# PSUM banks for batch 0's attention: two groups of four by turns in place of one ring of seven

## The chip, the core and the metric

The kernel runs on one core of one Trainium2 chip. The metric is the device time of one execution in microseconds (us): the median of the runs. Lower is better. The engines are called as in the profile: PE (TensorE), DVE (VectorE), ACT (ScalarE), POOL (GpSimd), SP (SyncE, which issues the transfers). PSUM, the memory that PE writes its products to, is used as eight banks, k0 to k7.

## What is computed

Attention over 8 batches of 8 heads (576 positions, 64 wide), and a feed-forward layer on its result:

```python
q_d, k_d, v_d = (t.reshape(B, H, S // 4, 4, D).mean(axis=3) for t in (q, k, v))
out_up = np.repeat(sm_attn(q_d, k_d, v_d), 4, axis=2)     # softmax attention on means of 4 positions
scores = np.where(abs(i - j) < 4, q @ k.T / 8, -1e9)      # and attention on the 7 nearest positions
out_local = softmax(scores) @ v
x = (out_up + out_local) as 4608 rows of 512              # rows: batch by batch; columns: heads
h = x @ w_in                                              # 512 -> 2048
out = (s * np.maximum(h, 0) ** 2 + b) @ w_out             # 2048 -> 512
```

A row of x needs all heads of its batch, so the feed-forward layer can't start on a batch before all of its attention is done.

## The kernel before

**The feed-forward part** takes 18 tiles of 256 rows (t) and 8 slices of 256 hidden columns (p). `gemm1(t, p)` writes 24 products of x with a slice of w_in into one bank (ph, L556 to L558: both factors are split in a high and a low part, and three of the four products are taken); ACT and DVE then make the squared result in two parts (L566 to L569), and `gemm2(t, p)` adds 12 products with a slice of w_out (po, L601 to L603). The steps run in the order of a list: t = 0 and 1 by turns for p = 0 to 6, then t = 2 for p = 0 to 6, then p = 7 of the three, then t = 3 to 17. A gemm2 is written two steps behind its gemm1. Tile t = 2 holds the end of batch 0 and the start of batch 1, so its first gemm1 needs the whole attention of batch 1.

**The weights** are 64-bit numbers, which ACT and DVE turn into a high and a low part in `convert` (L226 to L234). Slices p = 0 to 6 have a staging buffer each in turn; slice 7 (`load_quarter`, L211) comes in eight quarters: load, L226 on ACT, L227 to L230 on DVE, L231 on ACT, L234 on DVE. A quarter's load reuses the buffer of the quarter ahead, so it can't start before that quarter's L230.

**Attention of batches 0 to 2** goes by pairs of heads, four a batch, each in `first_unit`. A pair takes eight PSUM tiles in this order: sa (products of the averaged q and k, L303), sl twice (the near scores, one head each, L383 and L388), tp and tr (transposes, L322 to L327), up (L337, L339), ol twice (L431). On the way the softmax of sa goes over DVE L304, ACT L305, L307, L311, DVE L312, ACT L314; that of sl over DVE L393, L394, ACT L397, DVE L398 to L401 (batch 0: L401 on POOL), DVE L411 and ACT L414 four times; L434 on DVE adds ol and up into x. `split_x` (L542 on ACT, L543 on DVE) makes x's high and low part, xh and xl, for gemm1. A bank is handed on when the reader of its tile is done.

**Banks.** Each pair draws its tiles from a ring, the next tile from the next bank. Batch 0 uses one ring of k0 to k3 and k5 to k7 for all four pairs. The rings of batch 1 (k5, k6) and 2 (k5) are small, since gemm1 and gemm2 hold the others: ph of t = 0 is in k4, that of t = 1 in k7 for p under 7, po of t = 0, 1, 2 in k0 and k1, k2 and k3, k6 and k7.

**The order of the instructions** isn't the order in which the functions are called. A scheduler builds each engine's queue from a model of the run: it takes what its model has ready, the attention of batches 0 to 2 ahead of the rest (`tc.high_priority`). Each engine then runs its own queue strictly in order, so an instruction that waits holds back all that stand behind it on that engine. One changed bank thus moves instructions on all engines.

Of the kernel before, what the change touches and what calls it, by code (L numbers as in the profile page):

```python
# [62 lines left out]
def attention_ffn_kernel(ctx, tc, qk, vw_in, vr_in, vdm, qkn, vn, w_in, w_out, s_in, b_in, out):  # L63
# [8 lines left out]
    def bank(i, shape, name):  # L72
        return ps.tile(shape, F32, tag=f"k{i}", name=name)
# [109 lines left out]
    def clear(i):  # L183
        da, vm = room[i]["dg"], room[i]["sc"][:, 1536:1792]
        n = 2 * NG * P
        for j in range(0, n + QV, 488):
            nc.gpsimd.memset(da[:, j : min(j + 488, n + QV)], 0.0)
        nc.gpsimd.memset(vm, 0.0)
        diag[i] = (take(da, 0, [P, 2 * NG, P]), *blocks(da, n, vm))
# [431 lines left out]
    def banks(*ids):  # L621
        ring = itertools.cycle(ids)
        return lambda shape, name: bank(next(ring), shape, name)

    def load_ahead(i):
        for j in range(i, min(i + 3, EU)):
            load_pair(*units[j])
# [7 lines left out]
    sb_b = cst.tile([P, 1], F32, name="sb_b")  # L635
    nc.sync.dma_start(sb_b, bass.AP(b_in.tensor, b_in.offset, [[0, P], [1, 1]]))
    clear(1)
    bk = banks(0, 1, 2, 3, 5, 6, 7)
    for hp in range(HP):
        load_ahead(hp)  # L640
        if hp > 1:
            clear(hp)
        with tc.high_priority(offset=400):
            for _ in first_unit(0, hp, bk):
                pass
    split_w(0)
    load_w(1)
# [122 lines left out]
```

## Time and profile before

| | |
| --- | --- |
| device time, median of 3 runs | 971.38 us (971.03 to 973.79) |
| the profiled execution | 972.49 us, its span 970.7 us |
| busy share of the span: PE, DVE, ACT, POOL | 97%, 66%, 49%, 43% |
| granted PE clock | 1.00 of full in the whole span |
| DVE busy from 30 to 69.2 us | 37.97 of 39.2 us |
| PE busy from 30 to 69.2 us | 27.95 of 39.2 us |
| PE busy from 69.2 to 160 us | 90.80 of 90.8 us |

The program has two stretches. Up to about 69 us all engines work on batch 0's attention, and on the first weights; PE waits for the others. After that PE runs the feed-forward part, with the attention of later batches strewn in, almost without a gap to the end. In the timeline rows the columns are start, duration, engine, line, operation, tiles (written <- read), and in brackets the idle time of the engine just ahead and what ended it. Durations of neighbours on one engine overlap by some hundredths to tenths of a microsecond, so what a row costs its queue is the distance to the next start. The profile counts an fp32 product of PE as two (12 rows of ol are x24).

### The profile page before, as it was taken

How to read it: one execution, taken by the hardware profiler on the slowest of the kernel's cores; microseconds unless marked ns; L12 is line 12 of the kernel's file. 1: busy time of each engine (PE TensorE's matmuls, PEld its weight loads, DVE VectorE, ACT ScalarE, POOL GpSimd, SP SyncE). 2: the span in 40 equal slices, each digit the busy share in tenths (PEclk: the TensorE clock that was granted, in tenths of full speed). 3: DMA queues.
4: the chain of work that ended last, by engine and by line, in shares of the span. 5: the costliest groups of instructions: out<-in, count | busy, mean ns of one | idle time of the engine just before them, and what ended most of it. 6: DMA issues, size and time to landing. Idle time of an engine off the chain costs nothing.

```text
span 970.7 us, 18541 instructions
## 1 busy us (share of the span) xinstructions
PE 938.7 (97%) x7316; PEld 843.4 (87%) x7316; DVE 637.7 (66%) x1175; ACT 475.0 (49%) x1141; POOL 418.0 (43%) x455
## 2 busy tenths in 40 slices
PE   5769999999999999999999999999999999999998
PEld 4559988888999999998888899989899999998987
DVE  5999996864567878787787878787878521211121
ACT  5878775553754453545363545453635433333231
POOL 9421011101066686776868786867676200000000
PEclk9999999999999999999999999999999999999999
DMA  9736512112243232323241424242412000000000
GB/s 316 261 121 210 172 60 78 49 42 73 101 134 113 77 110 72 102 70 133 67 136 66 135 68 131 72 134 69 136 55 76 1 22 1 23 1 22 1 23 22
DMA packets 32103, 86.26 MB, mean 89 GB/s; under 512 B 3344, under 2 KB 7952, under 8 KB 32016
## 3 DMA queue, kind: packets, MB, share of 16 engines
q1 hardware_dynamic: 32016, 85.08, 26.6%
q8 instruction: 57, 0.93, 0.4%
q14 instruction: 30, 0.25, 0.1%
HBM read 75.63 MB, written 9.44 MB: 88 GB/s over the span
## 4 chain that ended last, share of the span: by engine, by line
PE 74%; DVE 9%; DMA 8%; POOL 5%; ACT 2%; issue 2%; SPq 0%; DVEq 0%; ACTq 0%; POOLq 0%
PE ph L556 11%; PE ph L557 11%; PE ph L558 11%; PE po L603 11%; PE po L601 11%; PE po L602 11%; DMA tqk<-in_qk_dram 3%; POOL pr L466 3%; POOL acc L488 3%; DMA wst<-in_moe_w_out_dram 2%; PE sa L303 2%; DVE bias L579 1%; PE up L339 1%; PE ol L431 1%; DMA lqk<-in_qkn_dram 1%
## 5 line engine op out<-in xcount | busy, mean ns | idle before, releaser
L556 PE MATMUL ph<-xh,wi 128*128 128x256 f32 x1152 | 325.4, 283 | 3.7 <-ACT xh L542 2.5
L557 PE MATMUL ph<-xl,wi 128*128 128x256 f32 x1152 | 323.9, 281 | 0.0
L558 PE MATMUL ph<-xh,wi 128*128 128x256 f32 x1152 | 323.6, 281 | 0.0
L466 POOL TENSOR_TENSOR pr<-lqk 128x576 f32<-128x576 f32 x140 | 201.2, 1461 | 73.2 <-DMA lqk<-in_qkn_dram 29.2
L556 PEld LDWEIGHTS ph<-xh,wi 128*128 128x128 f32 x1152 | 217.5, 189 | 11.2 <-ACT xh L542 2.8
L557 PEld LDWEIGHTS ph<-xl,wi 128*128 128x128 f32 x1152 | 217.4, 189 | 5.4 <-issue 0.2
L558 PEld LDWEIGHTS ph<-xh,wi 128*128 128x128 f32 x1152 | 217.6, 189 | 0.3
L566 ACT ACTIVATE ph<-ph 128x512 f32<-128x512 f32 x144 | 83.8, 582 | 229.0 <-PE ph L558 223.2
L601 PE MATMUL po<-wo,gh 128*128 128x512 f32 x456 | 180.7, 396 | 0.0
L602 PE MATMUL po<-wo,gh 128*128 128x512 f32 x456 | 180.5, 396 | 0.0
L603 PE MATMUL po<-wo,gl 128*128 128x512 f32 x456 | 177.9, 397 | 0.0
L569 DVE TENSOR_TENSOR gl<-ph,gh 128x512 fp32r<-128x512 f32 x114 | 77.8, 683 | 115.8 <-ACT gh L568 115.5
L488 POOL TENSOR_TENSOR acc<-acc,pv 128x576 f32<-128x576 f32 x80 | 114.4, 1430 | 57.1 <-DVE acc L488 29.5
L468 DVE TENSOR_REDUCE st<-pr 128x9 f32<-128x576 f32 x140 | 105.9, 757 | 37.7 <-POOL pr L466 35.4
L292 POOL TENSOR_TENSOR dq<-vq 64x64 f32<-64x64 f32 x58 | 22.8, 393 | 197.4 <-PE up L337 195.3
L603 PEld LDWEIGHTS po<-wo,gl 128*128 128x128 f32 x456 | 85.7, 188 | 17.6 <-issue 0.2
L487 DVE TENSOR_TENSOR pv<-lv,st 128x576 f32<-128x576 f32 x120 | 87.5, 747 | 18.8 <-POOL acc L488 18.4
L601 PEld LDWEIGHTS po<-wo,gh 128*128 128x128 f32 x456 | 85.7, 188 | 15.9 <-ACT gh L568 0.6
L602 PEld LDWEIGHTS po<-wo,gh 128*128 128x128 f32 x456 | 85.7, 188 | 15.8
L568 ACT CAST gh<-ph 128x512 fp32r<-128x512 f32 x114 | 66.9, 587 | 64.3 <-PE po L602 62.4
L567 ACT ACTIVATE ph<-ph 128x512 f32<-128x512 f32 x144 | 83.7, 582 | 3.2
L602 PE MATMUL po<-wo,gb 128*128 128x512 f32 x120 | 47.1, 392 | 0.0
(149 smaller groups left out, 1239.3 us busy)
## 6 DMA issues: line engine op xcount, KB each, us to landing
tqk<-in_qk_dram SPq DMA_DIRECT2D x30, 584.0 KB, 4.1
lqk<-in_qkn_dram SPq DMA_DIRECT2D x20, 768.0 KB, 4.2
lv<-in_vn_dram SPq DMA_DIRECT2D x20, 480.0 KB, 3.4
out_dram<-os SPq DMA_DIRECT2D x17, 512.0 KB, 3.1
wst<-in_moe_w_in_dram SPq DMA_DIRECT2D x7, 1024.0 KB, 6.5
wst<-in_moe_w_out_dram SPq DMA_DIRECT2D x7, 1024.0 KB, 5.3
tvd<-in_vdm_dram SPq DMA_DIRECT2D x29, 160.0 KB, 2.9
tvr<-in_vr_dram SPq DMA_DIRECT2D x29, 128.0 KB, 3.1
```

The source lines that it names most:

```text
L466: nc.gpsimd.tensor_tensor(pr, lqk[:, 0:CH], lqk[:, CH + o : 2 * CH + o], ALU.mult)
L468: nc.vector.tensor_reduce(ls[:, :, o], pr, AX.X, ALU.add)
L487: nc.vector.tensor_tensor(pv, lv[:, o : o + CH], w, ALU.mult)
L488: (nc.vector if o % 3 == 1 else nc.gpsimd).tensor_tensor(acc[:, :, h], acc[:, :, h], pv, ALU.add)
L556: nc.tensor.matmul(ph[:, j], wi[p][:, 0, k, f], xh[:, k], start=(k == 0), stop=False)
L557: nc.tensor.matmul(ph[:, j], wi[p][:, 0, k, f], xl[:, k], start=False, stop=False)
L558: nc.tensor.matmul(ph[:, j], wi[p][:, 1, k, f], xh[:, k], start=False, stop=(k == NK - 1))
L566: nc.scalar.activation(ph, ph, AF.Relu)
L567: nc.scalar.activation(ph, ph, AF.Square)
L601: nc.tensor.matmul(po[m], gh[:, j, ms], wo[p][:, 0, j], start=first, stop=False)
L602: nc.tensor.matmul(po[m], gh[:, j, ms], wo[p][:, 1, j], start=False, stop=False)
L603: nc.tensor.matmul(po[m], gl[:, j, ms], wo[p][:, 0, j], start=False, stop=last)
```

## The change

Batch 0's pairs 0 and 2 draw their eight tiles from a ring of k0 to k3, pairs 1 and 3 from one of k4 to k7. A pair has four banks in place of seven, but shares them with one other pair only, and k4, unused by batch 0 before, is taken as well. No instruction is added or removed.

```diff
-    bk = banks(0, 1, 2, 3, 5, 6, 7)
+    bks = [banks(0, 1, 2, 3), banks(4, 5, 6, 7), banks(0, 1, 2, 3), banks(4, 5, 6, 7)]
     for hp in range(HP):
 ...
-            for _ in first_unit(0, hp, bk):
+            for _ in first_unit(0, hp, bks[hp]):
```

The queues change from their first few instructions to the last gemm1 of t = 2; behind that they are the same, instruction by instruction. Three places follow; numbers behind a name tell buffers apart, and x3 means three equal rows.

**PE, around the first gemm1.** `ph<-xh,wi` (L556) is its first product. In the rows before, tp, tr, up and ol with the names pd, ptr, dq, db are those of batch 1's first pair; ol<-flat is batch 0's last.

```order
L322 MATMUL tp<-ident,pd 80x96
L325 MATMUL tp<-ident,pd 80x96 x2
L327 MATMUL tr<-ident,pd 64x96 x3
L337 MATMUL up<-ptr,dq 128x144
L339 MATMUL up<-ptm,dq 128x144 x2
L431 MATMUL ol<-flat 64x96 x12
L556 MATMUL ph<-xh,wi 128x256
L431 MATMUL ol<-db,tvw 64x96 x12
L557 MATMUL ph<-xl,wi 128x256
```

The same place with the change:

```order
L431 MATMUL ol<-flat 64x96 x12
L383 LDWEIGHTS idb
L383 MATMUL sl<-maskb,idb 128x192
L388 MATMUL sl<-tqk 32x32 x24
L556 MATMUL ph<-xh,wi 128x256
L322 MATMUL tp<-ident,pd 80x96
L325 MATMUL tp<-ident,pd 80x96 x2
L556 MATMUL ph<-xh,wi 128x256
L557 MATMUL ph<-xl,wi 128x256
```

Batch 1's first pair has only sa and sl ahead of the first gemm1 now; its tr, up and ol stand further back among gemm1 and gemm2, and the pairs after it are all later too.

**PE, the end of batch 1's last pair** (up_1925, ol_1931 and ol_1951 are its tiles; ph_2127 is gemm1 of t = 1, p = 6). Before, it is strewn among the feed-forward products:

```order
L601 MATMUL po_1068<-wo_1581,gh_1919 128x512
L337 MATMUL up_1925<-ptr_1885,dq_139 128x144
L339 MATMUL up_1925<-ptm_1883,dq_139 128x144 x2
L602 MATMUL po_1068<-wo_1581,gh_1919 128x512
...
L556 MATMUL ph_2127<-xh_751,wi_1698 128x256
L431 MATMUL ol_1931<-db_146,tvw_1088 64x96 x6
L557 MATMUL ph_2127<-xl_752,wi_1698 128x256
L558 MATMUL ph_2127<-xh_751,wi_1698 128x256
L556 MATMUL ph_2127<-xh_751,wi_1698 128x256
L431 MATMUL ol_1951<-db_146,tvw_1088 64x96 x6
```

With the change (ph_2179 is the first gemm1 of t = 2, sa_2334 the first tile of batch 2; the rows ahead of these are the last gemm2 of p = 6 with sa_1755 and sl_1766 of the pair among them):

```order
L383 LDWEIGHTS idb_120
L383 MATMUL sl_1825<-maskb_122,idb_120 128x192
L388 MATMUL sl_1825<-tqk_1082 32x32 x24
L322 MATMUL tp_1875<-ident_75,pd_1753 80x96
L325 MATMUL tp_1875<-ident_75,pd_1753 80x96 x2
L327 MATMUL tr_1876<-ident_75,pd_1753 64x96 x3
L337 MATMUL up_1925<-ptr_1885,dq_139 128x144
L339 MATMUL up_1925<-ptm_1883,dq_139 128x144 x2
L431 MATMUL ol_1931<-db_146,tvw_1088 64x96 x6
L431 MATMUL ol_1951<-db_146,tvw_1088 64x96 x6
L303 MATMUL sa_2334<-kd_2318,dq_139 96x144 x3
L556 MATMUL ph_2179<-xh_2173,wi_705 128x256
```

All gemm2 of p = 0 to 6 now stand ahead of it, and from sl_1825 to the first gemm1 of t = 2 no product of the feed-forward part stands between the pair's steps.

**DVE, the same pair.** es_2024 to es_2054 are quarters of slice 7; sm_1765 and pl_1764 belong to the pair, x_794 is batch 1's x. Before, two quarters stand in front of the pair's last steps:

```order
L411 STREAM_TRANSPOSE pt_1888<-pl_1764 128x384
L569 TENSOR_TENSOR gl_1985<-ph_1959,gh_1984 128x512
L227 TENSOR_SCALAR es_2014<-es_2014 128x256
...
L227 TENSOR_SCALAR es_2024<-es_2024 128x256
L228 TENSOR_SCALAR es_2024<-es_2024 128x256
L229 SCALAR_TENSOR_TENSOR es_2024<-wst_2022,es_2024 128x256
L230 SCALAR_TENSOR_TENSOR es_2024<-wst_2022,es_2024 128x256
L569 TENSOR_TENSOR gl_2110<-ph_2084,gh_2109 128x512
L434 TENSOR_TENSOR x_794<-ol_1931,ups_1929 128x288
```

With the change, later quarters stand there, and one of them between L399 and L400:

```order
L399 TENSOR_SCALAR sm_1765<-sm_1765 128x12
L227 TENSOR_SCALAR es_2044<-es_2044 128x256
L400 RECIPROCAL sm_1765<-sm_1765 128x12
L228 TENSOR_SCALAR es_2044<-es_2044 128x256
L401 TENSOR_TENSOR pl_1764<-pl_1764,sm_1765 128x384
L229 SCALAR_TENSOR_TENSOR es_2044<-wst_2042,es_2044 128x256
L276 TENSOR_REDUCE qd_2603<-tqk_1718 128x144
L411 STREAM_TRANSPOSE pt_1888<-pl_1764 128x384
...
L227 TENSOR_SCALAR es_2054<-es_2054 128x256
L434 TENSOR_TENSOR x_794<-ol_1931,ups_1929 128x288
```

The quarter es_2034 stands in the same way between the pair's L304 and its L398 (not shown), so three quarters are threaded through the pair where two stood behind its L411.

## The prediction

> **What bounds the kernel now.** I read the busy times by stretch first, then the timelines of PE, DVE and ACT at the two places where the queues change most. By stretch (engines PE, weight load, DVE, ACT, POOL):
>
> ```profile
> 30.00:69.20 39.20, 27.95 (x391) 22.72 (x381) 37.97 (x87) 31.95 (x81) 10.99 (x13) 1.00 0.50 163
> 69.20:160.00 90.80, 90.80 (x905) 81.43 (x904) 82.17 (x156) 66.92 (x145) 10.66 (x18) 1.00 0.43 141
> 160.00:240.00 80.00, 78.24 (x736) 66.91 (x736) 51.46 (x97) 36.47 (x87) 7.67 (x12) 1.00 0.16 50
> 240.00:970.70 730.70, 724.87 (x4979) 658.84 (x4977) 448.09 (x797) 323.08 (x778) 361.88 (x344) 1.00 0.22 73
> ```
>
> From 30 to 69.2 us DVE bounds (37.97 of 39.2), from 69.2 PE does (90.80 of 90.8, and 99% after 160). So the end is set by two things: when PE can begin the feed-forward part, and every hole in PE behind that. DVE stays close behind PE until 160 us (82.17 of 90.8): what PE starts earlier, DVE must deliver earlier.
>
> The start, on PE:
>
> ```profile
> 64.57 0.58 PE L556 MATMUL ph<-xh,wi 128*128 128x256 f32 x1 [2.50 <-ACT xh L542]
> 67.06 2.24 PE L431 MATMUL ol<-db,tvw 128*64 128x96 f32 x24 [1.91 <-ACT db L414]
> 69.24 0.58 PE L557 MATMUL ph<-xl,wi 128*128 128x256 f32 x1
> 69.62 0.42 PE L558 MATMUL ph<-xh,wi 128*128 128x256 f32 x1
> 72.39 0.36 PE L556 MATMUL ph<-xh,wi 128*128 128x256 f32 x1
> 72.95 0.28 PE L557 MATMUL ph<-xl,wi 128*128 128x256 f32 x1
> 73.07 0.28 PE L558 MATMUL ph<-xh,wi 128*128 128x256 f32 x1
> ```
>
> gemm1 really begins at 69.24: its second product stands behind ol of batch 1's first pair. Its operand xl came from DVE at 65.72 + 1.21 = 66.93:
>
> ```profile
> 24.59 0.58 DVE L411 STREAM_TRANSPOSE pt<-pl 128x384 f32<-128x384 f32 x1 [3.20 <-POOL pl L401]
> 63.36 0.56 DVE L411 STREAM_TRANSPOSE pt<-pl 128x384 f32<-128x384 f32 x1
> 63.85 0.64 DVE L234 TENSOR_TENSOR wo<-es,wo 128x512 fp32r<-128x512 f32 x1
> 64.42 0.41 DVE L228 TENSOR_SCALAR es<-es 128x512 int32<-128x512 int32 x1
> 64.75 0.68 DVE L229 SCALAR_TENSOR_TENSOR es<-wst,es 128x512 int32<-128x512 int32 x1
> 65.35 0.44 DVE L434 TENSOR_TENSOR x<-ol,flat 128x288 f32<-128x288 f32 x1
> 65.72 1.21 DVE L543 TENSOR_TENSOR xl<-x,xh 128x1024 fp32r<-128x1024 f32 x1
> ```
>
> Start to start, a step on 512 columns costs DVE 0.57 to 0.60 us (L229, L230, L234) or 0.33 (L227, L228).
>
> The second place, the first gemm1 of t = 2, which needs all of batch 1's x:
>
> ```profile
> 159.02 0.39 PE L603 MATMUL po<-wo,gl 128*128 128x512 f32 x1
> 159.25 0.28 PE L556 MATMUL ph<-xh,wi 128*128 128x256 f32 x1
> 160.30 0.28 PE L557 MATMUL ph<-xl,wi 128*128 128x256 f32 x1
> ```
>
> PE came to it without a hole; its real start is 160.30 (four po stand between its first two products), while xl of batch 1 was there at 157.0 (below).
>
> **The change, part by part.** It adds and removes no instruction, so all its cost is order. I sum against the profiled execution (972.49 us, 1.11 above the median of 971.38), by one number: T, when PE starts gemm1 of t = 2 (its L557), 160.30 before. What stands behind T is the same but for what moved across it.
>
> *Start of the feed-forward part.* In DVE's queue 18 instructions that stood ahead of the first xl stand behind it now: of batch 1's first pair one L393 and L394 (0.27 each), L398 (0.46), L399 (0.08), L400 (0.14), L401 (0.48), L411 (0.49); an L276 (0.67); of the weights three L234, one L229 and two L230 (six at 0.60) and two each of L227 and L228 (four at 0.33). Together 7.8 us, by the same distances in DVE's timeline (24.59 and 63.36 to 65.72 are a part of it). Two come ahead (L230, L234: 1.2). So xl is 6.6 us sooner if DVE waits as long as before. It should wait less: the 3.20 us ahead of L411 were a wait for POOL, and six steps of weights and softmax now stand in front of that L411; I let them fill 2.0 of it (bounds 0 and 3.2). xl comes at 66.93 - 6.6 - 2.0 = 58.3. Batch 1's ol no longer stands between, so PE begins at 58.3 in place of 69.24 (57.1 to 60.3): 10.9 us earlier. The other wait there is for xh on ACT (1.05 us ahead of xl in its chain), which moves with x.
>
> *PE's way to t = 2.* Before, 160.30 - 69.24 = 91.1 us. Now more work stands on it: the first pair's tp, tr, up and ol, and the last gemm2 of p = 6, of which 20 products used to stand behind. Rows for these:
>
> ```profile
> 149.34 0.41 PE L337 MATMUL up<-ptr,dq 128*128 128x144 f32 x2
> 149.58 0.66 PE L339 MATMUL up<-ptm,dq 80*128 80x144 f32 x4
> 149.98 0.49 PE L602 MATMUL po<-wo,gh 128*128 128x512 f32 x1
> 152.15 0.72 PE L431 MATMUL ol<-db,tvw 128*64 128x96 f32 x12
> 152.80 0.38 PE L557 MATMUL ph<-xl,wi 128*128 128x256 f32 x1
> 164.85 0.90 PE L303 MATMUL sa<-kd,dq 128*96 128x144 f32 x6
> 165.49 0.49 PE L601 MATMUL po<-wo,gh 128*128 128x512 f32 x1
> ```
>
> up is 0.64, ol 0.65 a half, tp and tr some 0.5 (six products, by the same rows), together 2.4; 20 po at 0.234 are 4.7 (159.02 to 159.25 shows one); sa of batch 2, now ahead too, 0.65 to 0.7. So without a hole T would be 58.3 + 91.1 + 2.4 + 4.7 + 0.7 = 157.2, and behind T 5.4 us less is left. The weights on the way should be just in time: the last piece of p = 6 has 6.9 us less in front of it on DVE by the same count, and PE wants it some 14 us sooner, where there were 4 to 5 us to spare. I take a hole of 0 there (0 to 2).
>
> *The hole ahead of t = 2.* This is what the change costs. Batch 1's last pair now runs at the end of this stretch, and from its second sl on PE has nothing else. Its steps and the quarters of slice 7 before, on DVE:
>
> ```profile
> 152.66 0.29 DVE L227 TENSOR_SCALAR es<-es 128x256 f32<-128x256 f32 x1 [1.10 <-ACT es L226]
> 154.72 0.45 DVE L434 TENSOR_TENSOR x<-ol,ups 128x288 f32<-128x288 f32 x1
> 156.06 0.96 DVE L543 TENSOR_TENSOR xl<-x,xh 128x768 fp32r<-128x768 f32 x1 [0.20 <-ACT xh L542]
> 158.11 0.29 DVE L227 TENSOR_SCALAR es<-es 128x256 f32<-128x256 f32 x1 [1.09 <-ACT es L226]
> 163.07 0.29 DVE L227 TENSOR_SCALAR es<-es 128x256 f32<-128x256 f32 x1 [1.77 <-ACT es L226]
> 168.04 0.29 DVE L227 TENSOR_SCALAR es<-es 128x256 f32<-128x256 f32 x1 [2.53 <-ACT es L226]
> 174.33 0.29 DVE L227 TENSOR_SCALAR es<-es 128x256 f32<-128x256 f32 x1 [1.93 <-ACT es L226]
> ```
>
> and on ACT:
>
> ```profile
> 135.76 0.38 ACT L307 ACTIVATE pd<-sa,dmx 96x144 f32<-96x144 f32 x1
> 142.46 0.53 ACT L397 ACTIVATE pl<-pl 128x384 f32<-128x384 f32 x1 [0.76 <-DVE pl L394]
> 147.73 2.08 ACT L414 COPY db<-pt 32x384 f32<-32x384 f32 x4
> 155.20 0.83 ACT L542 CAST xh<-x 128x768 fp32r<-128x768 f32 x1 [0.56 <-DVE x L434]
> ```
>
> The pair's sa stands 6.9 us of PE work ahead of t = 2 (sa 0.7, two sl 1.1, eight po 1.9, tp and tr 0.5, up 0.6, ol 1.3, sa of batch 2 0.7), so it starts at 157.2 - 6.9 = 150.3. From there the shortest chain is sa 0.9, L304 0.6, L305 0.2, three L307 1.1, the second sl 0.6 (its bank was sa's), L393 and L394 0.6, L397 0.5, L398 to L401 1.4, L411 0.6, L414 2.1, ol 1.3, L434 0.5, L542 0.8, L543 1.0: 12.2, so T can't be under 162.5. Three quarters are threaded through it on DVE, and each holds the queue until its load and L226 are done, with the pair's next step behind it. Before, DVE stood 1.10, 1.09, 1.77, 2.53 and 1.93 in front of such an L227, 1.7 in the mean; three make 5.1. T = 150.3 + 12.2 + 5.1 = 167.6, a hole of 10.4 us in all. The bounds: the waits hidden beside ACT's steps (162.5), or the quarters' own four DVE steps (1.3 a quarter) on the chain as well (171.5).
>
> *Restart.* The only chunks that came behind a long wait of PE are those at 69.62 to 72.39: 13 steps of 0.213 us, against 0.12 from 72.95 on. The whole slow run was about 16 products, 1.5 us lost. No row of before shows PE slow again, but no later gap is of several us either. I take 1.5 (0 to 1.5), by the nearest row. The Trainium skill (TensorE: Matmul & The Clock Gate, Part 1) says that the array falls back to half clock after an idle window of about 3.4 us and needs as long to warm; by that this would be up to 1.7, an estimate from the page.
>
> *Refill.* Behind T the first gemm2 of t = 2 must wait for ACT and DVE with no older gemm2 as cover. Before, PE had a hole at the same place, for the same sl of batch 2:
>
> ```profile
> 177.10 0.26 PE L383 MATMUL sl<-maskb,idb 128*128 128x192 bf16 x1 [1.06 <-DVE pl L394]
> ```
>
> I set one against the other: 0 (-1 to 2).
>
> *The sum.* (167.6 - 160.3) - 5.4 + 1.5 + 0 = +3.4 us: 972.49 + 3.4 = 975.9 for such an execution, 974.8 beside the median. The early start is worth -8.5 (10.9 less the 2.4 moved behind it); hole and restart give back 11.9.
>
> **The rivals.** A measurement of this kernel can tell about 0.3%, 2.9 us, from no change.
>
> *Faster: the last pair is hidden.* If DVE comes through with few waits and the quarters' loads arrive while ACT works, T nears its floor; if also the pair's sa starts sooner (T 157.2 is the extreme, with no hole), the end is 157.2 - 160.3 - 5.4 = -8.5: 962.9. It decides at T = 161.3, where -2.9 is reached. For it: PE is at that sa with nothing missing, DVE has 9 us idle from 69 to 160. Against: the floor of 162.5 is counted from rows, and holds unless PE gets to the pair earlier. At the floor, without a restart loss, the end is 2.2 - 5.4 = -3.2. Chance 0.15.
>
> *No change: the hole eats just what the start won.* T from 161.3 to 167.1. The waits of two quarters rather than three, T = 165.9: +1.7, 973.1. Chance 0.37.
>
> *Slower, as forecast*, with T above 167.1. Chance 0.48. In it is the case that the change doesn't start the feed-forward part earlier: if ACT holds x back, so that PE begins as late as 66, sa of the last pair starts at 158, T is near 174, and the end +9. ACT was busy 31.95 of 39.2 us there, DVE more; I give this 0.08 of the 0.48.
>
> **How the numbers follow.** The likeliest is slower: 974.8. Its own range, T from 167.1 to 171.5, is 974.3 to 978.7. The range for 8 in 10 leaves out the fully hidden pair and the start that doesn't come: low 967.0 (T near 162.5 with refill for nothing), high 979.5 (T = 171.5 with the refill's 2 in part). Faster 0.15, same 0.37, slower 0.48.
>
> **What would show it.** Right: the first L557 near 58 us; ol of batch 1's first pair among later chunks; at 150 to 168 us holes in PE, ended by DVE L394, ACT L414 and ACT xh L542, with DVE waiting for ACT es L226 between L399 and L400; slow chunks at the start of t = 2. Wrong: a first L557 later than 61; or T under 161, with chunks of the feed-forward part running up to it; or holes between 60 and 130 us for weights, which I set at nothing.

## The result, and the profile after

The changed kernel takes 981.2 us in the median of 4 runs (978.44 to 982.56) where the kernel before takes 971.82 in the same set: the ratio is 1.009, with an interval of 1.0062 to 1.0117. It is slower by 9.4 us, where 3.4 were forecast, and outside the forecast's range (967.0 to 979.5). Ratios, here and below, leave out the one disturbed execution (1042 us, of both_w_hp) and can differ by 0.1% from the quotient of two medians. The profiled execution took 980.62 us with a span of 978.8; before, it was 972.49 and 970.7. So 8.1 of the 9.4 us can be read in the two traces.

By stretch (same columns as before: PE, weight load, DVE, ACT, POOL, granted clock, DMA):

```profile
30.00:59.30 29.30, 22.19 (x376) 17.51 (x376) 28.55 (x67) 26.10 (x70) 4.83 (x6) 0.53 0.55 185
59.30:150.90 91.60, 90.82 (x809) 81.46 (x809) 83.25 (x156) 64.85 (x132) 9.99 (x18) 0.98 0.41 138
150.90:169.60 18.70, 10.45 (x156) 8.37 (x154) 11.91 (x32) 10.58 (x31) 2.90 (x6) 0.73 0.33 110
169.60:242.20 72.60, 69.84 (x677) 60.20 (x678) 46.02 (x84) 32.30 (x76) 6.24 (x12) 0.95 0.14 44
242.20:978.80 736.60, 729.82 (x5010) 663.19 (x5008) 449.69 (x799) 324.51 (x780) 362.46 (x344) 1.00 0.22 73
```

From 59.3 to 150.9 us PE is again busy for 90.82 of 91.6 us. Then come 18.7 us in which it works for 10.45 only, and no other engine is full either (DVE 11.91): a chain of waits. Before, there was no such stretch. On PE, the start:

```profile
59.34 0.58 PE L557 MATMUL ph<-xl,wi 128*128 128x256 f32 x1
59.72 0.41 PE L558 MATMUL ph<-xh,wi 128*128 128x256 f32 x1
...
62.28 0.34 PE L558 MATMUL ph<-xh,wi 128*128 128x256 f32 x1
62.45 0.28 PE L556 MATMUL ph<-xh,wi 128*128 128x256 f32 x1
```

gemm1's second product, which stood at 69.24, is at 59.34, and batch 1's first pair no longer stands ahead of it. The slow products are here too: they follow one another by 0.21 us up to 62.28, and by 0.12 from there. The stretch that costs, again on PE, from batch 1's last sa to the second gemm1 of t = 2 (178.43):

```profile
150.88 0.90 PE L303 MATMUL sa<-kd,dq 128*96 128x144 f32 x6
...
155.44 0.24 PE L383 MATMUL sl<-maskb,idb 128*128 128x192 bf16 x1 [0.98 <-ACT pd L307]
...
157.03 0.28 PE L322 MATMUL tp<-ident,pd 96*80 96x96 f32 x1 [0.80 <-ACT pd L314]
...
158.87 0.82 PE L337 MATMUL up<-ptr,dq 128*128 128x144 f32 x2 [1.15 <-ACT ptr L332]
...
165.20 2.19 PE L431 MATMUL ol<-db,tvw 128*64 128x96 f32 x24 [4.55 <-ACT db L414]
167.32 1.40 PE L303 MATMUL sa<-kd,dq 128*96 128x144 f32 x6
169.65 0.38 PE L557 MATMUL ph<-xl,wi 128*128 128x256 f32 x1 [0.82 <-DVE xl L543]
169.87 0.29 PE L558 MATMUL ph<-xh,wi 128*128 128x256 f32 x1
...
175.49 0.34 PE L383 MATMUL sl<-maskb,idb 128*128 128x192 bf16 x1 [2.17 <-DVE pl L394]
...
176.56 0.79 PE L601 MATMUL po<-wo,gh 128*128 128x512 f32 x1
...
178.43 0.41 PE L556 MATMUL ph<-xh,wi 128*128 128x256 f32 x1
```

T is 169.65. Ahead of it PE stands idle for 0.98, 0.80, 1.15, 4.55 and 0.82 us, each time for a step of batch 1's last pair (pd, ptr, db, xl). Behind T there is a second gap, of 2.17 us ahead of batch 2's second sl, and the products behind that are slow, those of ph at 0.21 a step up to 181.6. The ones at T, from 169.87 on, are not. Why the pair takes so long is seen on DVE:

```profile
151.81 0.60 DVE L304 TENSOR_REDUCE dmx<-sa 96x3 f32<-96x432 f32 x1 [0.70 <-PE sa L303]
...
158.95 0.17 DVE L399 TENSOR_SCALAR sm<-sm 128x12 f32<-128x12 f32 x1
160.00 0.30 DVE L227 TENSOR_SCALAR es<-es 128x256 f32<-128x256 f32 x1 [0.88 <-ACT es L226]
160.23 0.22 DVE L400 RECIPROCAL sm<-sm 128x12 f32<-128x12 f32 x1
...
162.48 0.56 DVE L411 STREAM_TRANSPOSE pt<-pl 128x384 f32<-128x384 f32 x1
...
165.61 0.42 DVE L234 TENSOR_TENSOR wo<-es,wo 128x256 fp32r<-128x256 f32 x1 [2.26 <-ACT wo L231]
166.58 0.29 DVE L227 TENSOR_SCALAR es<-es 128x256 f32<-128x256 f32 x1 [0.55 <-ACT es L226]
166.79 0.45 DVE L434 TENSOR_TENSOR x<-ol,ups 128x288 f32<-128x288 f32 x1
```

And on ACT:

```profile
152.98 0.43 ACT L226 ACTIVATE es<-wst 128x256 f32<-128x256 f32 x1 [2.33 <-DMA wst<-in_moe_w_out_dram]
...
153.96 0.20 ACT L305 ACTIVATE dmx<-dmx 96x3 f32<-96x3 f32 x1
...
159.54 0.43 ACT L226 ACTIVATE es<-wst 128x256 f32<-128x256 f32 x1 [0.76 <-DMA wst<-in_moe_w_out_dram]
...
163.08 2.07 ACT L414 COPY db<-pt 32x384 f32<-32x384 f32 x4 [2.11 <-DVE pt L411]
```

Between the pair's L399 and L400 stands a quarter's L227, which waits for L226 on ACT, and that one for its load from DRAM (0.76 us). Behind L411 the quarter's L234 waits 2.26 us for ACT, which is busy with the pair's own L414 from 163.08 to 165.15, and the pair's L434 stands behind the next L227. A quarter holds the pair up on ACT as well: the pair's L304 is done at 152.41, but its L305 starts at 153.96 only, behind a quarter's L226 that has waited 2.33 us for its load.

The two traces can be set side by side by four marks on PE: the start (first L557), T, the first gemm1 of t = 3, and the last product. Work is what PE has queued between two marks, at the steps at which products follow one another without a wait or a change of form (0.118 us for ph, 0.234 for po, some 0.6 to 0.7 for a tile of sa, sl, up or ol, as in the prediction); lost is the rest of the time.

| | before | after | forecast of the difference | difference |
| --- | --- | --- | --- | --- |
| start | 69.24 | 59.34 | -10.9 | -9.9 |
| work from the start to t = 3 | 156.8 | 158.8 | +2.4 | +2.0 |
| lost from the start to T | 3.6 | 15.5 | +10.4 | +11.9 |
| lost from T to t = 3 | 5.7 | 8.6 | +1.5 | +2.9 |
| from t = 3 (235.31, 242.18) to the last product | 731.6 | 732.9 | 0 | +1.3 |
| sum | | | +3.4 | +8.2 |

### The profile page after: what moved, and what is told of

It is laid out like the page before. It is cut to its first block, busy times and chain, and to the rows that moved or that the text cites. A ratio compares the mean times of both kernels' runs of the same rounds, so it can differ in the third digit from the quotient of the medians.

```text
span 978.8 us, 18539 instructions
## 1 busy us (share of the span) xinstructions
PE 938.4 (96%) x7316; PEld 843.5 (86%) x7316; DVE 639.2 (65%) x1175; ACT 474.8 (49%) x1141; POOL 413.3 (42%) x455
## 4 chain that ended last, share of the span: by engine, by line
PE 77%; DVE 8%; DMA 6%; POOL 4%; ACT 3%; issue 1%; DVEq 0%; ACTq 0%; SPq 0%; POOLq 0%
PE ph L556 12%; PE ph L557 12%; PE po L601 12%; PE ph L558 12%; PE po L602 12%; PE po L603 12%; POOL acc L488 2%; POOL pr L466 2%; DMA tqk<-in_qk_dram 2%; PE sa L303 2%; DMA wst<-in_moe_w_in_dram 1%; DMA lqk<-in_qkn_dram 1%; PE up L339 1%; PE ot L498 1%; DMA flat<-in_qk_dram 1%
## 5 line engine op out<-in xcount | busy, mean ns | idle before, releaser
L556 PE MATMUL ph<-xh,wi 128*128 128x256 f32 x1152 | 326.5, 284 | 3.9 <-ACT xh L542 1.9
L557 PE MATMUL ph<-xl,wi 128*128 128x256 f32 x1152 | 324.4, 282 | 0.8 <-DVE xl L543 0.8
L556 PEld LDWEIGHTS ph<-xh,wi 128*128 128x128 f32 x1152 | 218.4, 190 | 11.3 <-DVE gb L569 2.8
L557 PEld LDWEIGHTS ph<-xl,wi 128*128 128x128 f32 x1152 | 218.2, 189 | 6.2 <-DVE xl L543 1.3
L292 POOL TENSOR_TENSOR dq<-vq 64x64 f32<-64x64 f32 x58 | 19.9, 342 | 218.8 <-PE up L337 216.6
L603 PEld LDWEIGHTS po<-wo,gl 128*128 128x128 f32 x456 | 85.7, 188 | 18.1 <-issue 0.2
L487 DVE TENSOR_TENSOR pv<-lv,st 128x576 f32<-128x576 f32 x120 | 87.6, 748 | 20.5 <-POOL acc L488 19.9
```

The source lines that it names most:

```text
L487: nc.vector.tensor_tensor(pv, lv[:, o : o + CH], w, ALU.mult)
L556: nc.tensor.matmul(ph[:, j], wi[p][:, 0, k, f], xh[:, k], start=(k == 0), stop=False)
L557: nc.tensor.matmul(ph[:, j], wi[p][:, 0, k, f], xl[:, k], start=False, stop=False)
L603: nc.tensor.matmul(po[m], gl[:, j, ms], wo[p][:, 0, j], start=False, stop=last)
```

## The experiments

Two theories stood against each other. *Hole theory*: banks matter only through the order that they lead to; the loss is the hole ahead of t = 2, because batch 1's last pair now stands 7 us of PE work ahead of T and its chain, with quarters of weight slice 7 threaded through it, takes longer. *Bank theory*: batch 0's pairs now hold bank 4, where gemm1 has its ph, and that costs. To these came two for parts of the loss: the *clock* (PE is slow behind a hole), and *interleaving* (products of an sl strewn between those of the feed-forward part). In the table lost and work are as above; the products that experiments only added are not counted as work.

| kernel | median, us | start | lost to T | lost T to t = 3 | t = 3 to end |
| --- | --- | --- | --- | --- | --- |
| before | 971.8 | 69.2 | 3.6 | 5.7 | 731.6 |
| changed | 981.2 | 59.3 | 15.5 | 8.6 | 732.9 |
| q_behind | 976.5 | 59.9 | 13.5 | 11.1 | 730.7 |
| r4_3 | 981.9 | 59.0 | 18.1 | 7.8 | 731.8 |
| r43q | 979.4 | 61.3 | 12.3 | 9.5 | 730.4 |
| last4 | 983.7 | 64.3 | 10.2 | 12.1 | 730.5 |
| ap0_23 | 972.7 | 62.2 | 10.1 | 6.1 | 730.7 |
| b_q | 971.5 | 68.9 | 2.7 | 6.1 | 730.6 |
| warm1b | 984.0 | 60.0 | 15.0 | 14.1 | 730.1 |
| warm1b_hp | 980.5 | 62.3 | 15.2 | 7.8 | 729.0 |
| bp0_23 | 982.1 | 66.9 | 4.2 | 15.9 | 730.9 |
| bp0_hp | 974.0 | 64.6 | 4.9 | 9.7 | 729.3 |
| both | 970.8 | 58.6 | 9.0 | 9.8 | 730.0 |
| both_w_hp | 971.5 | 59.4 | 8.9 | 9.2 | 729.2 |

The kernel before had medians of 970.8 to 972.0 beside these. Medians are of 4 to 12 runs, the other columns of one execution each, so a column tells a microsecond or two, not tenths: the start alone lies between 58.6 and 62.3 in seven kernels whose queues on PE and DVE are the same up to it, but for three tr on PE in some (the changed one, q_behind, ap0_23, warm1b, warm1b_hp, both, both_w_hp).

**q_behind: the quarters out of the pair.** In load_quarter, ahead of the load (and split_w(7) one step later in the program, so that this x exists):

```diff
+        if (op, i) == ("o", 0):
+            nc.vector.tensor_copy(st.bitcast(F32)[0:1, 0, 0:1], xt[1][0:1, HP - 1, 0:1])
         nc.sync.dma_start(st.rearrange("p f t -> p (f t)"), src)
```

> The changed kernel, but the four wo quarters of weight slice 7 can't start before batch 1's last pair has written the first half of its x (a copy of one element of x into the quarter's staging tile goes ahead of the first of these loads). Nothing of the quarters is then left between the pair's steps on DVE; PE's order up to T (the first gemm1 of t = 2, its L557) is the same. Hole theory (the time was lost because batch 1's last pair stands 7.1 us of PE work ahead of t = 2 while its chain took 18.8 us from its sa at 150.9 to T at 169.65, with the quarters threaded through it): by the prediction's term of 5.1 us for three quarters T comes near 164.5 and the time near 976. If the quarters only fill DVE's waits and the chain itself is long: T above 168.5, time 980 to 981. Bank theory (what costs is that batch 0's pairs now hold bank 4, where gemm1 has its ph, and banks 5 to 7 by fours): no change, 981.

Measured: 976.47 us, a ratio to before of 1.0046 (1.0027 to 1.0064), 4.7 less than the changed kernel. The pair's steps on DVE (lines behind 210 are two further down here: L395 is L393, L413 is L411, L436 is L434):

```profile
157.59 0.36 DVE L395 TENSOR_REDUCE sm<-sl 128x6 f32<-128x192 f32 x1 [0.73 <-PE sl L390]
...
161.68 0.57 DVE L413 STREAM_TRANSPOSE pt<-pl 128x384 f32<-128x384 f32 x1
165.75 0.46 DVE L436 TENSOR_TENSOR x<-ol,ups 128x288 f32<-128x288 f32 x1 [3.50 <-PE ol L433]
```

No quarter stands between them any more; what DVE waits for is PE (3.50 us for ol, which itself waits for ACT's L414). From sa (153.31) to T (168.16) the chain took 14.85 us in place of 18.77. So three quarters cost it 3.9, not the 5.1 of the forecast, and the pair alone is longer than the 12.2 that was counted. Step by step, by the rows of both traces, 1.5 of the 3.9 lie between L304 and L312, where ACT stood at a quarter's L226 in front of L305; 1.7 lie between L399 and L411, and 0.7 behind L411. DVE's waits in front of the three L227 in the changed kernel were 0.38, 0.88 and 0.55, 1.8 in all. Not all of the 3.9 is seen at the end of the profiled execution, which was the slowest of its six (979.42): it lost 1.9 us more ahead of sa, and 2.5 more behind T, where the quarters now stand.

**r4_3 and last4: other rings for batch 0.** The line with bks is another in each; r4_3:

```diff
-    bks = [banks(0, 1, 2, 3), banks(4, 5, 6, 7), banks(0, 1, 2, 3), banks(4, 5, 6, 7)]
+    bks = [banks(0, 1, 2, 3), banks(5, 6, 7)] * 2
```

last4, a part of the change alone:

```diff
-    bks = [banks(0, 1, 2, 3), banks(4, 5, 6, 7), banks(0, 1, 2, 3), banks(4, 5, 6, 7)]
+    bks = [banks(0, 1, 2, 3, 5, 6, 7)] * 3 + [banks(4, 5, 6, 7)]
```

> The changed kernel, but the second ring is banks 5 to 7 and not 4 to 7: batch 0's pairs no longer touch bank 4, where the first gemm1 has its ph. The first x of batch 0 is ready on DVE after about the same work (0.3 us less), and batch 1's last pair stands 11.1 us of PE work ahead of T in place of 7.1. Hole theory: the hole is 4 us shorter, one more us of attention stands behind the start: 977 to 978.5, with PE's start near 59. Bank theory: without bank 4 the loss is gone, 972 or less. If only the start counts and the hole is a follow-up of something else: 981 as the changed kernel.

> A part of the change alone: the ring of seven for pairs 0 to 2 as before, banks 4 to 7 for batch 0's last pair only. On DVE 5.6 us more work stands ahead of the first xl than in the changed kernel (1.0 less than before the change), and batch 1's last pair stands 15.8 us of PE work ahead of T. Hole theory: PE starts near 64 to 65, the hole is 18.8 - 15.8 = 3 us instead of 11.7, and the time comes to 973 to 978, between the two kernels, nearer to before. Bank theory: bank 4 is held by one pair, the last one, so nearly the whole loss stays: 979 to 981.

Measured: 981.85 (ratio 1.0095, 1.0079 to 1.011) and 983.66 (1.0119, 1.0102 to 1.0136), both above what hole theory expected (at most 978.5 and 978). Bank theory falls with r4_3: without bank 4 the loss is the same, where 972 was expected. That the hole only follows from something else is not ruled out here, since 981 was expected for that too; ap0_23 below bears on it. The fixed chain of 18.8 us falls as well. In r4_3 the pair's sa came 25.1 us ahead of T and it still was late, in last4 22.7. On DVE in r4_3:

```profile
158.47 0.29 DVE L227 TENSOR_SCALAR es<-es 128x256 f32<-128x256 f32 x1 [2.65 <-ACT es L226]
...
159.01 0.35 DVE L393 TENSOR_REDUCE sm<-sl 128x6 f32<-128x192 f32 x1
...
163.96 0.29 DVE L227 TENSOR_SCALAR es<-es 128x256 f32<-128x256 f32 x1 [1.10 <-ACT es L226]
164.17 0.57 DVE L411 STREAM_TRANSPOSE pt<-pl 128x384 f32<-128x384 f32 x1
...
170.49 0.29 DVE L227 TENSOR_SCALAR es<-es 128x256 f32<-128x256 f32 x1 [1.86 <-ACT es L226]
...
171.49 0.45 DVE L434 TENSOR_TENSOR x<-ol,ups 128x288 f32<-128x288 f32 x1
```

The more room the pair is given, the more quarters are put into it; here their L227 hold up its second L393, its L411 and its last L434 by 2.65, 1.10 and 1.86 us. last4 started at 64.3, as expected, lost 5.3 us less than the changed kernel up to T, and then 3.5 more behind T, of which bp0_hp below tells more.

**r43q: both edits.** r4_3 with the edit of q_behind.

> The kernel with batch 0 on banks 0 to 3 and 5 to 7 by turns (981.9 alone), and the wo quarters of slice 7 behind batch 1's last pair. In the kernel alone that pair stood 11.1 us of PE work ahead of T, yet its chain from sa to T took 25.1 us, and its second L393 and its L411 to L434 stood on DVE behind three L227 that waited 2.65, 1.10 and 1.86 us for their quarter. Quarter theory (the chain is as long as what is threaded into it, not a fixed 18.8): without them the chain comes to 14 to 17 us, as the 14.9 of the changed kernel with the same edit, T near 163 to 165 in place of 172.9, and the time to 973 to 976. If the chain is long for another reason (ACT, the two banks): 20 us or more, 979 to 982.

Measured: 979.41 (1.0088, 1.0064 to 1.0111), 2.4 less than r4_3. The chain came down from 25.1 to 19.9, not to 14 to 17: 5.1 us of what is left (151.6 to 156.7) is PE's own feed-forward work, queued ahead of the second sl, which costs nothing. What was lost up to T fell from 18.1 to 12.3. So the quarters hold up the pair in both kernels, by 3.9 and 5.2 us of chain, and without them some 8 to 9 us between sa and T are still lost. They are a part of the hole, not the hole.

**ap0_23: the pair comes earlier.** Batch 1's first pair gets two banks more, which gemm2 of t = 1 needs only later:

```diff
-    rings = {1: banks(5, 6), 2: banks(5), 3: banks(2, 3, 5)}
+    rings = {0: banks(5, 6, 2, 3), 1: banks(5, 6), 2: banks(5), 3: banks(2, 3, 5)}
-            yield from first_unit(*units[i], rings[min(i // HP + i // (EU - 2), 3)])
+            yield from first_unit(*units[i], rings[0 if i == HP else min(i // HP + i // (EU - 2), 3)])
```

> The changed kernel with batch 0's rings as they are in it, and one thing more: batch 1's first pair takes its tiles from banks 5, 6, 2 and 3 in turn, not 5 and 6 alone, so that its last tiles stand in banks 2 and 3 (which gemm2 of t = 1 needs only later) and batch 1's second pair can start some 20 us of PE work earlier. The early start is kept (the same 45.0 us of DVE work ahead of the first xl), and batch 1's last pair stands 20.6 us of PE work ahead of T, more than its chain of 18.8. Hole theory: no hole ahead of t = 2, T near 155 to 157, and the time near 964 to 969, faster than both kernels. Bank theory: batch 0 still holds banks 4 to 7, so 980 to 981. A third way: gemm2 of t = 1 waits for banks 2 and 3 and gives part of it back as a hole near 75 to 80 us: 970 to 975.

Measured: 972.68 (0.9998, 0.9983 to 1.0013): 8.5 us less than the changed kernel, and just the time of before, but 3.7 above the range that hole theory gave. By the table it starts 2.9 us later than the changed kernel, loses 5.4 less ahead of T and 2.5 less from T to t = 3. PE's waits in ap0_23 from 140 to 175 us (in total, times, longest):

```profile
PE sa L303 <- DVE x L434: 1.0, 1, 1.0
PE po L601 <- ACT gh L568: 0.9, 1, 0.9
PE sl L383 <- DVE pl L394: 0.8, 1, 0.8
PE ph L557 <- DVE xl L543: 0.6, 1, 0.6
```

Where the hole was there are 3.3 us of waits in all, 1.8 of them behind T (166.98), with batch 0 on banks 4 to 7 as in the changed kernel. That is the second thing against bank theory, and the main one for the hole. But it does not beat before: the start of this execution is 62.2, and 10.1 are lost up to T, 2.2 of them in waits for pd and gl at 73 to 76 us, and some 3 in slow products of ph behind these waits and behind the start.

**b_q: the quarters in the kernel before.** The edit of q_behind, in the kernel before.

> The kernel before with the one edit that took the wo quarters of slice 7 behind batch 1's last pair in the changed kernel. There the pair's sa stands 26.6 us of PE work ahead of T and PE never waits for it, so by the hole theory the quarters cost nothing here: 971.5 to 973, no difference from 972.0. If the 4.7 us that this edit gave the changed kernel were a gain of its own (the bias rows, DMA traffic, slice 7 arriving otherwise), it would come here as well: 967 to 968.

Measured: 971.50 (0.9998, 0.9984 to 1.0011): nothing. Where PE never waits for the pair the quarters are free; their price in the changed kernel comes with the pair's place.

**warm1b and warm1b_hp: the clock.** Sixteen products into the bank of the last pair's second ol, overwritten by it:

```diff
             ol = banks([P, S // 2], "ol")
+            for _ in range(16 if (b, hp, f) == (1, HP - 1, 1) else 0):
+                nc.tensor.matmul(
+                    ol, wi[0][:, 0, 0, 0:P], wo[0][:, 0, 0, 0 : S // 2], start=True, stop=True)
```

> The changed kernel plus 16 products that are thrown away (128 x 288, the bank of the last pair's second ol, overwritten by that ol), queued on PE between up and the first ol of batch 1's last pair, where PE stands idle for 4.55 us; nothing else is moved on PE. It prices the restart: in the changed kernel the 24 ol products behind that idle time took 2.19 us, sa 1.14 and the four products ahead of ph's next chunk 0.43 each, at a granted clock of 0.59 to 0.75. If the slow products come from the idle time (clock): the 24 ol products take 1.3 to 1.5 us and sa 0.65 to 0.9, T comes near 168.5 and the time to 977 to 980. If they are slow for another reason (operands from ACT, the switch between kinds of products): the same durations, T 169.5 to 170.5, and 981 to 982.

PE in warm1b (lines behind 427 are three further down; L427 are the added products):

```profile
161.68 3.91 PE L427 MATMUL ol<-wo,wi 128*128 128x288 f32 x16 [0.37 <-ACT ups L421]
165.95 1.21 PE L434 MATMUL ol<-db,tvw 128*64 128x96 f32 x24 [0.37 <-ACT db L414]
...
176.27 0.40 PE L605 MATMUL po<-wo,gh 128*128 128x512 f32 x1
176.51 0.39 PE L604 MATMUL po<-wo,gh 128*128 128x512 f32 x1
...
176.98 0.28 PE L559 MATMUL ph<-xh,wi 128*128 128x256 f32 x1
177.09 0.28 PE L560 MATMUL ph<-xl,wi 128*128 128x256 f32 x1
```

Against the changed kernel the 24 products of ol take 1.21 us in place of 2.19, po 0.234 a step in place of 0.43, ph 0.118 in place of 0.213: the slow products come from the idle time, which is filled ahead of ol, and behind T is 0.85 and 0.70 us in place of 2.17 in one piece. Yet the time was 983.98 (1.0124, 1.0102 to 1.0146), 2.8 more. T did not move (169.92: xl was last, as before), and behind it 5.5 us more were lost. A part of that is order: PE's queue now strewed sl of batch 2 between single products of ph, 10 changes in place of 3 (8 in the kernel before, counted in the same way). Seven changes more are some 2.5 us by the price of a turn found below, and right behind the last of them seven steps of po took 0.43 us each in place of 0.234, with PE never idle. warm1b_hp takes the strewn sl away, with priority for the products of batch 2's sl and ol:

```diff
+            with tc.high_priority() if b == 2 else contextlib.nullcontext():
+                nc.tensor.matmul(sl, idb, maskb, start=True, stop=False)
...
+            with tc.high_priority() if b == 2 else contextlib.nullcontext():
+                for gg in range(NG // 2):
...
```

> The changed kernel with the 16 thrown-away products in its hole (984.0 alone), and with batch 2's sl and ol products taken in one go: behind T the sl give way 3 times, as in the changed kernel itself, in place of 10. In the kernel alone the slow products behind the hole were gone (ol 1.21 us in place of 2.19, po 0.234 a step in place of 0.43, ph 0.118 in place of 0.213), the second gemm1 of t = 2 started 1.45 us sooner, and then 7.2 us more were lost behind it. Clock theory and interleave theory together: those 7 us go, and the restart's price is what is left against the changed kernel, 3 to 4 us: 977 to 978.5. If keeping PE busy gives nothing that lasts: 980.5 to 982. If the 7 us were no interleaving: 983 to 984.

Measured: 980.51 (1.009, 1.0072 to 1.0107), 3.5 less than warm1b, and 0.7 less than the changed kernel, which is no difference that can be told. From T to t = 3 it lost 7.8 us in place of warm1b's 14.1. Against the changed kernel the gain is there up to the second gemm1 of t = 2 (7.04 us from T in place of 8.78); behind it stand two waits that the changed kernel does not have there, 0.7 us for gl and 2.0 for ptr.

**bp0_23 and bp0_hp: interleaving.** The kernel before with the rings of ap0_23, without and with the priority.

> The kernel before (batch 0 on its ring of seven), and batch 1's first pair on banks 5, 6, 2 and 3. On DVE 2.2 us less stands ahead of the first xl than before, the first pair's ol no longer stands between gemm1's first products on PE, and batch 1's last pair stands 26.2 us of PE work ahead of T, more than any chain seen (14.9 to 25.1). Start theory (the time goes with the start of gemm1, as long as no hole opens ahead of t = 2): PE starts at 63 to 65 in place of 69.24, 1.9 us of work moves behind it, and the time is 968 to 970. If an earlier start is eaten somewhere on the way in any case (weights, x, later waits): 971.5 to 973.

> The kernel before with batch 1's first pair on banks 5, 6, 2 and 3 (982.1 alone), and with batch 2's sl and ol products given priority, so that PE takes them in one go: in PE's queue between the second gemm1 of t = 2 and the first of t = 3, products of an sl give way to products of the feed-forward 3 times in place of 10, those of an ol 4 times in place of 8; up to T nothing changes. In the kernel alone PE lost 10.5 us against its work in that stretch, 5.5 in the kernel before. Interleave theory (an sl product between two of the feed-forward costs some 0.3 us each time, which has nothing to do with banks or with the hole): the stretch loses 5 to 6, and the time comes to 976 to 978. If the stretch was slow for another reason (weights late, the granted clock, batch 2's waits): 981 to 982.

Measured: 982.09 (1.0107, 1.0087 to 1.0127), a miss of 12 us, and 974.02 (1.003, 1.0017 to 1.0042), 2 us under the range expected. Ahead of T little was lost in either (4.2 and 4.9, against 3.6 before). PE in bp0_23:

```profile
232.62 0.25 PE L388 MATMUL sl<-tqk 64*32 64x32 f32 x2
232.79 0.38 PE L556 MATMUL ph<-xh,wi 128*128 128x256 f32 x1
233.11 0.24 PE L388 MATMUL sl<-tqk 64*32 64x32 f32 x2
```

A pair of sl products and one of ph take 0.49 us, where 0.118 and two times 0.0115 (48 rows in 0.55 us) would be 0.14: each turn costs 0.35, seven of them 2.4 us; four of ol cost 0.4 each. The Trainium skill (TensorEngine Tiling (Array Packing), Tiling Modes) says that a change of the tiling mode drains the engine; these rows agree in that such changes cost time, and put 0.35 us on two of them. In bp0_hp the same sl runs in one go (line 389 is 388 there):

```profile
223.60 0.62 PE L389 MATMUL sl<-tqk 64*32 64x32 f32 x48
```

From T to t = 3 it lost 9.7 us in place of 15.9: 4.0 us of turns, 1.7 of a wait of up for ptr that went as well, and some slow products.

**both and both_w_hp: the repairs together.** The changed kernel with the edits of ap0_23 and q_behind; and this with the priority, and with 8 products more in gemm2 (mark[2, 0] is the last product of the first gemm1 of t = 2):

```diff
+        if (t, p) == (2, 0):
+            with tc.issue_after(getattr(mark[2, 0], "ins", mark[2, 0])):
+                for _ in range(8):
+                    nc.tensor.matmul(
+                        po[0], wi[0][:, 0, 0, 0:P], wo[0][:, 0, 0], start=True, stop=True)
```

> The changed kernel with both repairs: batch 1's first pair on banks 5, 6, 2 and 3 (972.7 alone) and the wo quarters of slice 7 behind batch 1's last pair (976.5 alone). Hole theory: with the first repair 3.7 us were still lost between that pair's sa and T and 2.4 behind T; without the quarters about 1 and 1 to 2 stay, 968.5 to 971, faster than both kernels. If the two repairs take the same time away (after the first there is no hole left): 972 to 973.5.

> The changed kernel with all repairs: batch 1's first pair on banks 5, 6, 2 and 3, the wo quarters of slice 7 behind batch 1's last pair (970.8 with these two), 8 thrown-away products (128 x 512, into gemm2's own bank ahead of its first product) between the first gemm1 of t = 2 and batch 2's second sl, where PE waited 2.0 us and then ran slow from 169.4 to 174.4, and batch 2's sl and ol in one go (3 switches in place of 8). The slow run there cost 2.1 us in ph and some 0.8 in po, the switches some 2: 966 to 968, faster than both kernels. If either is given back at a later wait: 969 to 971.

Measured: 970.82 (0.9996, 0.9982 to 1.0009) and 971.50 (1.0007, 0.9991 to 1.0022). Neither beats the kernel before by anything that can be told, and both_w_hp misses its 966 to 968. both starts 10.7 us sooner than before and ends level. In both_w_hp the slow products behind T are gone, but a wait of 1.3 us for gh follows at 177 and 13 steps of ph are slow behind that one.

## Why the prediction was wrong

The direction and the mechanism were right in the main: an early start, paid for by a hole ahead of t = 2 where batch 1's last pair stands, with DVE in front of L400 waiting for a quarter's L226, as the forecast said. ap0_23 shows it by taking most of the hole away. The step that failed is the count of the hole's chain ("From there the shortest chain is ... 12.2"), and with it the refill behind T, put at 0 because before had a gap there too: the chain took 14.85 us without any quarter, and the terms behind T came to 2.9 us more than before in place of 1.5. Two of the signs named were off. Of the holes ahead of T only the one for L414 was among those named (the others ended with pd, ptr and xl), and the slow products of ph stand at the second gemm1 of t = 2, not at the first. Nearly all sizes were wrong to one side:

- *Start* (58.3 forecast): 59.34, since xl was there at 59.28 and not at 58.3. 1.0 us, within what this start varies by.
- *PE's way to t = 2* (157.2 without a hole, sa of the last pair at 150.3): sa at 150.88. No hole for weights between, as forecast. Moved work 2.0 in place of 2.4.
- *The hole* (a chain of 12.2 + 5.1 from sa to T): 18.77. q_behind splits it otherwise: 3.9 for the quarters, 14.85 for the pair. The chain of 12.2 left out L276 (0.67 between the pair's L401 and L411); it took the second sl and L397 at their shortest, where each stood 0.4 us behind something on its own engine; and it took ol at full speed (1.3, where it took 2.2 behind the idle time; with ol fast, in warm1b, the chain was only 0.35 shorter). The quarters' term had its mechanism half right: three L227 were to wait 1.7 us each on DVE, and they waited 1.8 in all; the rest was a wait on ACT ahead of L305 and the quarters' own steps. That the two errors are of opposite sign is luck: T = 169.65 lay within the bounds given (162.5 to 171.5), 2.05 above the value taken.
- *Restart* (1.5, at most 1.5): the slow products behind the hole and behind the gap at 173 to 175 cost some 4 us in the trace (ol 1.0, sa 0.4, sl and po 1.3, 16 steps of ph 1.5). But it is no term to be added: with the slow ol and those behind T taken away (warm1b_hp), 0.7 us came back in the median, which is within the noise.
- *Refill* (0): "I set one against the other" took the gap of before (1.06) for that of the changed kernel, with no row for how much of it the older gemm2 had covered. There was a gap of 2.17 us, and no products of an older gemm2 to cover it, because 20 of them now stood ahead of T. In the kernels with all of p = 6 ahead of T, some 2 to 5 us were lost between T and the second gemm1 of t = 2; in before and b_q, 0.2 and -0.1. With the restart it came to 2.9 in place of 1.5.
- *Behind t = 3* (nothing): 1.3. PE's queue is the same there, and this stretch lies between 729.0 and 732.9 in the 14 executions. It may be spread; it was not tested.

Of the 6.0 us by which the forecast fell short, the traces hold 4.8: start 1.0, moved work -0.4, the way to T 1.5, from T to t = 3 1.4, behind it 1.3. The rest is that the profiled execution after was under its median and the one before above it.

The range failed since its upper end took the upper bound of one term and left the others near their values. The terms that were uncertain here (hole, restart, refill, start) all hang on queues in which everything waits for the step ahead of it, and all came out on the same side.

The rival with a hidden pair was wrong too: it was to bring 962.9. In the six kernels with neither the hole nor the 10 changes of sl (they have 3 to 8) the first gemm1 of t = 3 comes at 235.3 (before), 234.6 (b_q), 237.0 (ap0_23), 235.9 (both), 236.1 (both_w_hp) and 237.6 us (bp0_hp), whether PE starts at 58.6 or at 69.2; with the hole it was 242.2. Where the early start goes in both and ap0_23 can be seen (gaps for pd and gl at 70 to 76 us, slow products behind them, a gap behind T), but whether one thing stands behind these is open. Open is also what the banks alone would do with the order left as it was: that was not tried.

## What to carry to other kernels

When a change only reorders, look for the unit of work that is pushed up against its deadline, and count its chain with all that the scheduler will put between its steps on each in-order engine; the more room a chain has, the more is threaded into it. Where several uncertain terms hang on the same queue, add their bounds on the same side. And an earlier start is worth its microseconds only as far as every later supplier can move with it.

## What the runs showed of the hardware

- PE was slow behind shorter gaps than expected. In the kernel both:

```profile
165.17 0.62 PE L390 MATMUL sl<-tqk 64*32 64x32 f32 x48
167.79 0.34 PE L385 MATMUL sl<-maskb,idb 128*128 128x192 bf16 x1 [2.00 <-DVE pl L396]
168.86 0.79 PE L603 MATMUL po<-wo,gh 128*128 128x512 f32 x1
...
170.73 0.41 PE L558 MATMUL ph<-xh,wi 128*128 128x256 f32 x1
...
174.36 0.36 PE L560 MATMUL ph<-xh,wi 128*128 128x256 f32 x1
```

  PE is idle for 2.00 us, between two tiles of sl, and all products from 167.79 to 174.36 are slow. The Trainium skill (TensorE: Matmul & The Clock Gate, Part 1) gives an idle window of about 3.4 us. The idle time here is shorter. From the last ph ahead of the gap (164.86) to the first po behind it (168.86) are 4.0 us, with little but the two tiles of sl between them, so it may be that products on small tiles count for little; no run here was made to test that. Two more traces point the same way. In ap0_23 ph ran slow from 76.57 us on, where the idle times ahead were 0.94 and 1.22 us with a tile of sl between them. In warm1b seven steps of po took 0.43 us each from 237.14 us on with no idle time at all, right behind seven turns of sl and ph.
- The record of the granted clock can't be relied on between traces: before's shows 1.00 from 60 to 75 us, where steps of ph took 0.213 us (from 69.83 to 72.39); in the changed kernel the same steps, from 59.72 to 62.28 us, go with a record of 0.50. Steps of equal products tell the clock.
- Products on 64x32 tiles strewn among products on the whole array cost 0.35 us a turn (bp0_23).
